# Seven block products in place of eight for x·w1, and sums that start from x in PSUM

## The chip, the cores and the metric

The kernel runs on one core of one Trainium2 chip. The metric is device microseconds of one execution; a single core runs it, so it is also the slowest core. Lower is better.

## The reference, cut to what matters

One transformer layer with two parallel branches on the same normalised input, all in fp32: S = 2048 tokens, D = 576, a hidden width F of 4608, 32 heads of 18.

```python
xn = layernorm(x)
q, k, v = split_heads(xn @ wqkv)                 # 576 -> 3 * 576
logits[s, w] = q[s] . k[s - 2 * w] * scale       # w = 0..7, masked where s - 2 * w < 0
A = (softmax(logits) @ v[s - 2 * w]) @ wo
B = relu(xn @ w1) @ w2                           # 576 -> 4608 -> 576
out = x + A + B
```

Nearly all of the multiplications are in `xn @ w1` (called h below), `relu(h) @ w2` (the second product), q/k/v and wo.

## The kernel before

**Precision.** Every fp32 operand of a matmul is split in two numbers of TensorE's format (fp32r): a high part, a copy that ScalarE makes, and a low part, the rest, subtracted by VectorE (helper `two`, L144). A product is then three products: high·high, high·low, low·high. D = 576 is four blocks of 128 rows and 64 rows left over. The left-over rows' high and low parts stand above one another in one block of 128, so that they take two matmuls where a full block takes three. The 14 pairs of blocks are the list `TERMS` (L326).

**Tokens.** They are dealt out in two phases (even and odd tokens), each of 8 tiles of 128, or 4 blocks of 256. A tile of x is loaded, normalised (`stats`, `norm`), turned on TensorE and split (`make_xt`, `transpose_split`); four tiles of the second phase are turned on VectorE and through DRAM instead (`norm_turned`, `xt_a`, `xt_f`, `xt_s`).

**The main loop** (L771) goes over `slots` (L540): phase, chunk of three F tiles (C = 3, 12 chunks), token block, F tile; 288 slots in all. In a slot:

- `h_mm` makes h for one F tile and one token block two slots ahead (LAG = 2): 14 matmuls of 128x128 by 256 tokens into a PSUM bank. `h_out` (L556) writes relu's high part by ScalarE (L563) and its low part by VectorE (L566) to SBUF.
- `o_mm` (L584) is the second product: for each of the two token tiles three products by two column halves (256 and 320 columns), so 12 matmuls, which accumulate over the three F tiles of a chunk in PSUM.
- After the third F tile `o_out` adds the PSUM sum to x in SBUF on VectorE (L620). After the last chunk the tile goes out.

All matmuls of the main loop are recorded at the helper `mm`, L113, and told apart by the tile that they write: `ph` is h, `po` the second product, `pm` q/k/v and wo (and a few others).

**Weights** are loaded on SP's queue to staging tiles and split ahead of use (`w1_task`, `w2_task`, `wq_tasks`, `wo_tasks`, `split_task`, `run_splits`; splits at L148 and L152); w1 and w2 are read from DRAM once per phase.

**Attention.** In four units of 8 heads per phase, `qkv_tile` runs 14 matmuls of 432 columns per token tile into `pm`, and ScalarE copies k, v and q out (L397 to L399). The first 7 places of k and v come from the neighbouring partition by DMA (the halo, L403). The rest of a unit is VectorE work in long instructions of 1152 columns (L428, L431, L458, L465), put in a queue `bg` and given out between other VectorE work by `run_bg` (L483), which compares two running sums of estimated PE and VectorE time. The result is turned on VectorE and through DRAM (`wo_a`, `wo_f`), split (`wo_s`), multiplied by wo (`wo_b`: 28 matmuls per token tile into `pm`) and added to x on VectorE (L529).

**Order of the work.** There is no scheduler at run time: each engine runs its instructions in program order and waits by semaphores. The program order is written out by hand for the head (L693 to L768) and follows from tables of slot numbers after that (`todo`, `todo_late`, `plan`). At the start h_terms runs the first products in pieces, as the parts of x and w1 become ready, and GpSimd makes some of the low parts (`by_pool`).

Of the kernel before, what the change touches and what calls it, by code (L numbers as in the profile page):

```python
# [17 lines left out]
P = 128  # L18
NPH = 2
NI = 8  # L20
NTB = 4
# [4 lines left out]
C = 3  # L26
LAG = 2
EPS = 1e-5

UNIT0, UNIT_STEP, WO_AT = 7, 26, 12  # L30

XT_STEPS = (
    (-6, 0, 1, 2, 4, 7),
    (-5, 1, 2, 3, 5, 8),
    (-3, 2, 3, 4, 6, 10),
    (3, 4, 5, 6, 8, 11),
)
WO_STEPS = (0, 1, 3, 4, 6, 7, 9, 10)
HEADW = (-9, -8, -7, -6, -5, -4)
FIRST = 4  # L40

HEAD = (
    (4, 0, 'stats', 6, False, True),
    (4, 1, 'norm', 6, True),
    (4, 1, 'stats', 7),
    (4, 1, 'norm', 7),
    (5, 1, 'xt', 6),
    (6, 0, 'xt', 7),
)
HALVED = 5  # L50
HALO = ((0, 112), (112, 127))
WARM = 24


@with_exitstack
def tile_body(ctx: ExitStack, tc: tile.TileContext, x, wqkv, wo, w1, w2, out):
# [5 lines left out]
    NF = F // P  # L62
    NCH = NF // C
    KT = 4
# [4 lines left out]
    SPC = NTB * C  # L69
    SPP = NCH * SPC  # L70
# [3 lines left out]
    consts = pool("consts", 1)  # L74
    xp = pool("xp", 11)
    xtp = pool("xtp", NTB)
    qop = pool("qop", 1)
    kp = pool("kp", 1)
    vp = pool("vp", 2)
    w1p = pool("w1p", C + 1)  # L80
    w2p = pool("w2p", C + 1)
    wqp = pool("wqp", 1)
    stp = pool("stp", 5)
    hp = pool("hp", LAG + 2)
# [3 lines left out]
    tmp = pool("tmp", 2)  # L88
    turned = pool("turned", 4, space=bass.MemoryType.DRAM)
    ps_o = pool("ps_o", 2, space=PSUM)  # L90
    ps_h = pool("ps_h", 2, space=PSUM)
    ps_m = pool("ps_m", 2, space=PSUM)

    f32 = lambda ap: ap.bitcast(F32)

    ident = consts.tile([P, P], F32, name="ident")
    make_identity(nc, ident)
    mhalf = consts.tile([P, 1], F32, name="mhalf")
    nc.gpsimd.memset(mhalf, -0.5)
    spare = consts.tile([P, 1], F32, name="spare")  # L100

    warm = ps_o.tile([P, 2, 512], F32, name="po")
    for _ in range(WARM):
        nc.tensor.transpose(warm[:, 0, 0:P], ident, ident)
# [3 lines left out]


    t = {"pe": 0.0, "dve": 0.0}  # L110

    def mm(o, l, r, start, stop, n):
        nc.tensor.matmul(o, l, r, start=start, stop=stop)  # L113
        t["pe"] += n / 2400.0 + 0.002

    def dve(n):
        t["dve"] += (n + 130) / 960.0


    tasks = deque()  # L120
    staged = deque()
    AHEAD = 3

    def split_task(step, load, split):
        tasks.append((step, load, split))

    def stage_more(ahead=AHEAD):
        while tasks and len(staged) < ahead:
            step, load, split = tasks.popleft()
            st = stp.tile([P, 640], F32, name="st")  # L130
            load(st)
            staged.append((step, split, st))

    def run_splits(n):
        nonlocal step_now
        while staged and staged[0][0] <= n:
            step_now, split, st = staged.popleft()
            split(st)
            stage_more()

    by_pool = set()
    step_now = None

    def two(hi, lo, src, n):  # L144
        if step_now == HEADW[0]:
            nc.vector.tensor_copy(hi, src)
        else:
            nc.scalar.activation(hi, src, AF.Copy)  # L148
        if step_now in by_pool:
            nc.gpsimd.tensor_tensor(lo, src, f32(hi), op=ALU.subtract)  # L150
        else:
            nc.vector.tensor_tensor(lo, src, f32(hi), op=ALU.subtract)  # L152
            dve(n)

    W1, W2, WQ, WO = {}, {}, {}, {}

    def w1_task(step, key, f):
        def load(st):
            c = slice(f * P, (f + 1) * P)
            nc.sync.dma_start(  # L160
                st[:, 0:512].rearrange("p (k c) -> p k c", k=KT),
                w1[0 : KT * P, c].rearrange("(k p) c -> p k c", p=P),
            )
            if key == (0, 0, 0):
                nc.scalar.dma_start(st[0:DR, 512:640], w1[KT * P : D, c])
                load_x(0, 1)
                nc.scalar.dma_start(st[DR:P, 512:640], w1[KT * P : D, c])
                return
            nc.sync.dma_start(st[0:DR, 512:640], w1[KT * P : D, c])
            nc.sync.dma_start(st[DR:P, 512:640], w1[KT * P : D, c])  # L170

        def split(st):
            w = w1p.tile([P, 2, 5 * P], F32R, name="w1t")
            two(w[:, 0, :], w[:, 1, :], st[:, :], 640)
            W1[key] = w

        split_task(step, load, split)

    def w2_task(step, key, f):
        def load(st):  # L180
            nc.sync.dma_start(st[:, 0:D], w2[f * P : (f + 1) * P, :])

        def split(st):
            w = w2p.tile([P, 2, D], F32R, name="w2t")
            two(w[:, 0, :], w[:, 1, :], st[:, 0:D], D)
            W2[key] = w

        split_task(step, load, split)

    def wq_tasks(steps, key, g):  # L190
        src = wqkv.rearrange("r (s c) -> r s c", s=3)

        def one(kt):
            def load(st):
                v = st[:, 0 : 3 * UD].rearrange("p (s c) -> p s c", s=3)
                c = slice(g * UD, (g + 1) * UD)
                if kt < KT:
                    nc.sync.dma_start(v, src[kt * P : (kt + 1) * P, :, c])
                else:
                    nc.sync.dma_start(v[0:DR], src[KT * P : D, :, c])  # L200
                    nc.sync.dma_start(v[DR:P], src[KT * P : D, :, c])

            def split(st):
                if kt == 0:
                    WQ[key] = wqp.tile([P, 10, 3 * UD], F32R, name="wq")
                w = WQ[key]
                two(w[:, kt, :], w[:, 5 + kt, :], st[:, 0 : 3 * UD], 3 * UD)

            return load, split

        for kt, step in enumerate(steps):
            split_task(step, *one(kt))

    def wo_tasks(steps, key):
        def one(kt):
            def load(st):
                if kt < KT:
                    nc.sync.dma_start(st[:, 0:D], wo[kt * P : (kt + 1) * P, :])
                else:
                    nc.sync.dma_start(st[0:DR, 0:D], wo[KT * P : D, :])  # L220
                    nc.sync.dma_start(st[DR:P, 0:D], wo[KT * P : D, :])

            def split(st):
                if kt == 0:
                    a = wqp.tile([P, 7, D], F32R, name="wq")
                    b = vp.tile([P, 3, D], F32R, name="v")
                    WO[key] = [a[:, k, :] for k in range(7)] + [b[:, k, :] for k in range(3)]
                w = WO[key]
                two(w[kt], w[5 + kt], st[:, 0:D], D)

            return load, split

        for kt, step in enumerate(steps):
            split_task(step, *one(kt))


    X, XT, XN, MR = {}, {}, {}, {}

    def load_x(ph, i):
        X[ph, i] = xp.tile([P, D], F32, name="x")  # L240
        if ph == i == 0:
            for c in slice(0, D2), slice(D2, D):
                nc.sync.dma_start(X[ph, i][:, c], x_v[ph, i][:, c])  # L243
            return
        (nc.scalar if (ph, i) == (0, 1) else nc.sync).dma_start(X[ph, i], x_v[ph, i])

    def stats(ph, i, parts=False, act=False):
        xt = X[ph, i]
        st = smp.tile([P, 2, 6], F32, name="bst")
        mv = smp.tile([P, 2], F32, name="mv", bufs=4)  # L250
        r = smp.tile([P, 1], F32, name="rstd", bufs=4)
        nm = smp.tile([P, 1], F32, name="nm", bufs=4) if act else mv[:, 0:1]
        MR[ph, i] = nm, r

        def sums():
            for h in range(2):
                nc.vector.bn_stats(st[:, h, :], xt[:, h * D2 : (h + 1) * D2])  # L257

        def rest():
            nc.vector.bn_aggr(mv, st)  # L260
            nc.vector.tensor_scalar(mv[:, 1:2], mv[:, 1:2], EPS, None, op0=ALU.add)
            if act:
                nc.gpsimd.tensor_scalar(nm, mv[:, 0:1], -1.0, None, op0=ALU.mult)
            nc.gpsimd.tensor_tensor(r, mv[:, 1:2], mhalf, op=ALU.pow)  # L264
            dve(700)

        if not parts:
            sums()
            rest()
        return sums, rest  # L270

    def norm(ph, i, act=False):
        nm, r = MR.pop((ph, i))
        xn = tmp.tile([P, 640], F32, name="xn", bufs=3)[:, 0:D]
        if act:
            nc.scalar.activation(xn, X[ph, i], AF.Identity, bias=nm)
            nc.scalar.activation(xn, xn, AF.Copy, scale=r)
        else:
# [4 lines left out]
    def transpose_split(src, hi, mix, lo, bank=None, parts=False):  # L283
# [28 lines left out]
        if not parts:  # L312
            for f in steps:
                f()
# [499 lines left out]
```

## Time and profile before

| | |
|---|---|
| Time, median of 3 runs | 1166.88 us (1165.29 to 1167.15) |
| Span of the profiled execution | 1163.8 us; no time of its own is listed, the median of the runs is 3.1 us more |
| Mean granted TensorE clock | 0.999 |
| Busy PE, VectorE (DVE), ScalarE (ACT), GpSimd (POOL) | 1155.9, 822.9, 308.1, 44.9 us |
| Bytes moved by DMA | 88.66 MB, mean 76 GB/s |

The span runs from the first to the last instruction of the profiled execution; what lies around it is in the time but not in the profile. PE stands for TensorE's matmuls and PEld for its weight loads, which overlap them. Several matmuls are in flight at once, so the mean length of one (277 ns for h) is longer than the distance from one to the next; paces are taken from runs of matmuls in the chain of work that ended last. A ScalarE or VectorE instruction overlaps the next one of its engine by about 0.1 us in the same way.

### The profile page before, as it was taken

The numbers are of one execution on the slowest core, as the hardware profiler recorded it, in microseconds if no ns is written. First come the engines' busy times: TensorE is split into PE (matmuls) and PEld (weight loads), VectorE is DVE, ScalarE is ACT, GpSimd is POOL, SyncE is SP. The second block draws the span as 40 slices with busy tenths as digits, with TensorE's granted clock in tenths as the row PEclk, the third lists the DMA queues.
The fourth block names the chain that finished last, engine by engine and source line by source line (L and its number), as shares of the span: only waits on it lengthen the run. The fifth ranks groups of instructions, "written<-read, shape, count | busy, mean of one in ns | idle before, by whom it ended". The sixth has DMA issues, their size and how long they took to land.

```text
span 1163.8 us, 21695 instructions
## 1 busy us (share of the span) xinstructions
PE 1155.9 (99%) x8916; PEld 1147.9 (99%) x8916; DVE 822.9 (71%) x1300; ACT 308.1 (26%) x747; POOL 44.9 (4%) x60
## 2 busy tenths in 40 slices
PE   8999999999999999999999999999999999999998
PEld 8999999999999999999999999999999999999998
DVE  7427885887687688876683288768858877887843
ACT  4422222131231212322433123222222312222210
POOL 2200100010000000000010001000100000000000
PEclk9999999999999999999999999999999999999999
DMA  6303221140321211365752113021312303113541
GB/s 184 98 23 85 65 55 53 40 112 1 94 76 34 82 32 52 96 151 116 175 170 66 46 53 94 22 77 36 92 34 62 110 1 101 44 32 97 123 100 63
DMA packets 149732, 88.66 MB, mean 76 GB/s; under 512 B 58512, under 2 KB 133264, under 8 KB 149632
## 3 DMA queue, kind: packets, MB, share of 16 engines
q1 hardware_dynamic: 146656, 78.54, 25.1%
q10 hardware_dynamic: 2976, 8.72, 2.6%
q8 instruction: 70, 1.15, 0.4%
q14 instruction: 30, 0.25, 0.1%
HBM read 67.90 MB, written 11.14 MB: 68 GB/s over the span
## 4 chain that ended last, share of the span: by engine, by line
PE 99%; issue 0%; DVE 0%; DMA 0%; POOL 0%; ACT 0%; SPq 0%; DVEq 0%; POOLq 0%
PE ph L113 39%; PE po L113 38%; PE pm L113 20%; PE pm L293 0%; DMA x<-in_x 0%; DVE x L626 0%; POOL rstd L264 0%; PE pm L294 0%; PE po L293 0%; ACT xT L298 0%; DVE xn L279 0%; DVE bst L257 0%; SPq L243 0%; DVEq L810 0%; PE ph L294 0%
## 5 line engine op out<-in xcount | busy, mean ns | idle before, releaser
L113 PE MATMUL ph<-xT,w1t 128*128 128x256 f32 x4018 | 505.0, 277 | 0.7 <-ACT xT L298 0.7
L113 PEld LDWEIGHTS ph<-xT,w1t 128*128 128x128 f32 x4018 | 486.8, 188 | 1.3 <-ACT xT L298 1.0
L113 PE MATMUL po<-w2t,hhi 128*128 128x256 f32 x2292 | 393.0, 293 | 0.0
L113 PEld LDWEIGHTS po<-w2t,hhi 128*128 128x128 f32 x2292 | 335.4, 188 | 1.1
L563 ACT ACTIVATE hhi<-ph 128x256 fp32r<-128x256 f32 x287 | 110.0, 384 | 582.2 <-PE ph L113 568.9
L113 PE MATMUL po<-w2t,hlo 128*128 128x256 f32 x1146 | 242.4, 292 | 0.0
L566 DVE SCALAR_TENSOR_TENSOR hlo<-ph,hhi 128x256 fp32r<-128x256 f32 x287 | 121.0, 422 | 164.5 <-ACT hhi L563 164.0
L113 PEld LDWEIGHTS po<-w2t,hlo 128*128 128x128 f32 x1146 | 188.9, 187 | 0.0
L620 DVE TENSOR_TENSOR x<-po,x 128x576 f32<-128x576 f32 x190 | 143.1, 757 | 60.1 <-PE po L113 57.2
L113 PE MATMUL pm<-wq,xT 128*128 128x432 f32 x896 | 185.5, 358 | 0.0
L113 PEld LDWEIGHTS pm<-wq,xT 128*128 128x128 f32 x896 | 163.8, 188 | 5.6
L428 DVE TENSOR_TENSOR pr<-qo,k 128x1152 f32<-128x1152 f32 x64 | 86.1, 1349 | 0.0
L431 DVE TENSOR_REDUCE lg<-pr 128x64 f32<-128x1152 f32 x64 | 85.1, 1343 | 0.0
L458 DVE TENSOR_TENSOR pr<-lg,v 128x1152 f32<-128x1152 f32 x64 | 84.7, 1350 | 0.0
L152 DVE TENSOR_TENSOR w2t<-st,w2t 128x576 fp32r<-128x576 f32 x72 | 55.8, 775 | 32.4 <-ACT w2t L148 32.3
L152 DVE TENSOR_TENSOR w1t<-st,w1t 128x640 fp32r<-128x640 f32 x70 | 58.9, 841 | 20.6 <-ACT w1t L148 20.5
L465 DVE TENSOR_TENSOR pr<-pr 128x288 f32<-128x288 f32 (+1 forms) x128 | 70.6, 601 | 0.0
L148 ACT ACTIVATE w2t<-st 128x576 fp32r<-128x576 f32 x72 | 49.3, 684 | 44.9 <-PE po L113 32.5
L397 ACT ACTIVATE k<-pm 128x144 f32<-128x144 f32 x64 | 18.7, 292 | 146.3 <-PE pm L113 146.3
L148 ACT ACTIVATE w1t<-st 128x640 fp32r<-128x640 f32 x71 | 52.1, 734 | 11.7 <-DMA k<-k 6.0
L434 POOL TENSOR_SCALAR_AFFINE_SELECT lg<-lg 1x512 f32<-1x512 f32 x8 | 9.9, 1234 | 809.6 <-DVE lg L431 809.6
L529 DVE TENSOR_TENSOR x<-pm,x 128x256 f32<-128x256 f32 (+1 forms) x32 | 13.1, 453 | 30.2 <-PE pm L113 30.2
(85 smaller groups left out, 470.0 us busy)
## 6 DMA issues: line engine op xcount, KB each, us to landing
st<-in_w SPq DMA_DIRECT2D x72, 288.0 KB, 3.1
st<-in_w SPq DMA_DIRECT2D x72, 256.0 KB, 3.2
st<-in_wqkv SPq DMA_DIRECT2D x32, 216.0 KB, 3.0
turned<-tr SPq DMA_DIRECT2D x64, 80.0 KB, 3.0
xn<-turned SPq DMA_DIRECT2D x16, 320.0 KB, 3.2
st<-in_w SPq DMA_DIRECT2D x142, 32.0 KB, 2.9
out<-x SPq DMA_DIRECT2D x15, 288.0 KB, 2.1
x<-in_x SPq DMA_DIRECT2D x14, 288.0 KB, 4.3
```

The lines of the kernel that those rows point to most:

```text
L113: nc.tensor.matmul(o, l, r, start=start, stop=stop)
L148: nc.scalar.activation(hi, src, AF.Copy)
L152: nc.vector.tensor_tensor(lo, src, f32(hi), op=ALU.subtract)
L397: nc.scalar.activation(k[:, W - 1 + i, :], pq[:, 1, :], AF.Copy)
L428: nc.vector.tensor_tensor(pr[i], q, window(k, i), op=ALU.mult)
L431: nc.vector.tensor_reduce(lg[:, i], pr.pop(i).rearrange(heads, d=Dh), axis=AX.X, op=ALU.add)
L458: nc.vector.tensor_tensor(pr[i].rearrange(heads, d=Dh), e, window(v, i).rearrange(heads, d=Dh), op=ALU.mult)
L465: nc.vector.tensor_tensor(o, z[:, 0:n], z[:, n : 2 * n], op=ALU.add)
L529: nc.vector.tensor_tensor(acc, po[h], acc, op=ALU.add)
L563: nc.scalar.activation(hi, pt, AF.Relu)
L566: nc.vector.scalar_tensor_tensor(lo, pt, 0.0, f32(hi), op0=ALU.max, op1=ALU.subtract)
L620: nc.vector.tensor_tensor(acc, whole, acc, op=ALU.add)
```

## The change

The work per phase is now 18 pairs of F tiles by two halves of the tokens (`G`: 72 groups in all). A group is 256 F columns by 512 tokens.

**h.** For a group, w1's 512 full rows are two halves of 256, and its 256 columns two F tiles; x's tokens are two blocks of 256. That is a product of 2x2 blocks. In all but the first four groups it is made by a Strassen (Winograd) scheme: seven products of sums of blocks, P1 to P7, instead of eight. The sums of w1's blocks (T1 to T4) are made for each pair by VectorE, the sums of x's blocks (S1 to S4) once for each phase and half. Partial results go on from product to product: P5 and P3 add up in bank bk3; P1, P6, P7 and P4 in bank bk2, which ScalarE copies to bank bkA after P1, where P2 adds to it, and to SBUF (SN2) after P6. P7's and P3's results are added to SBUF copies by VectorE. The 64 left-over rows are multiplied in the plain way, 2 matmuls for each of the four outputs, on top of P5, P2, P3 and P4. The first four groups (`classic`) are as before, 14 matmuls for each F tile and token block.

**Second product and wo.** For each token tile the sum over a pair's two F tiles (and, in four pairs of each phase, over a unit's part of wo) starts from x, which ScalarE has copied to PSUM, and ScalarE copies it back to SBUF after it. VectorE's adds of L620 and L529 go. wo's share of a unit is added when the unit is done (`WOP`), with the 16 left-over rows of each unit gathered and added with the last.

**Weights.** w1, w2, wqkv and wo are first copied within DRAM on GpSimd's queue, per pair or unit, and loaded from the copies. A pair's w1 blocks and sums take one of two SBUF buffers; in the pairs of `QP` the other one holds the q/k/v weights, and the next pair's w1 blocks are loaded and split after the last q/k/v matmul (`set_make` with `fine`).

**x of the second phase** is loaded to the attention's scratch tiles, normalised and turned on TensorE in groups 34 and 35, and split and summed in groups 35 and 36.

**Order.** A planner (`Order`) runs while the program is built: it keeps an estimated clock for each engine, and gives out ScalarE's and VectorE's instructions in the order in which they can start by these estimates, earliest due first. Attention instructions wait in a queue of their own and are placed on VectorE where they end at most 0.6 us after the start of the next known instruction. Each PE step forces what it needs.

The core of the diff:

```diff
+    def pick(self, eng):
...
+        if eng == DVE and self.back:
+            op = self.back[0]
+            r = self.ready(op)
+            if r is not None:
+                s = max(now, r)
+                if soon is None or s + op.dur <= soon[1] + self.SLACK:
+                    return op, s
+        return soon
...
+    def s_forms(h, slack):
...
+        a1 = dve(lambda: sub(z[S1], z[S3], z[S1], ALU.add), 512, [*RAW[h, 1], *XOK[h, 1]], slack)
+        a3 = dve(lambda: sub(z[S3], z[S2], z[S3]), 512, [a1, *raw, *XOK[h, 0]], slack + 0.6)
+        a2 = dve(lambda: sub(z[S2], z[S1], z[S2]), 512, [a3], slack + 1.2)
+        a4 = dve(lambda: sub(z[S4], z[S4], z[S2]), 512, [a2], slack + 1.8)
...
+    def terms(bank, ws, xs, start):
+        o = bank[:, 0:TBN]
+        for j, (wp, xp_) in enumerate(((0, 0), (0, 1), (1, 0))):
+            for k in range(len(ws[0])):
+                mm(o, ws[wp][k], xs[xp_][k], start and j == k == 0, False)
+
+    def rest(bank, m, f, xr):
+        w = wset(m)
+        for e in range(2):
+            mm(bank[:, 0:TBN], w[:, e, RR, f], xr, False, e == 1)
...
+    def pstep(g, name):
...
+        if name == "P5":
+            def f():
+                terms(bk3, slot(m, T1), sform(h, S1), True)
+                rest(bk3, m, 1, XR[h][:, 1])
+
+            t = pe(f, T8, [*ok[T1], *ok[RR], *XOK[h, "s"], *XOK[h, 1], *BANK["bk3"]])
+            BANK["bk3"] = [act(lambda: copy(SN5, b3), TBN, [t, *SNF[5]], 3)]
+        elif name == "P1":
+            t = pe(lambda: terms(bk2, slot(m, B11), aform(h, 0, 0), True), T6, [*ok[B11], *XOK[h, 0], *BANK["bk2"]])
+            BANK["bk2"] = [act(lambda: copy(bA, b2), TBN, [t, *BANK["bkA"]], 0.4)]
...
+        elif name == "P4":
+            def f():
+                terms(bk2, slot(m, T4), aform(h, 1, 1), False)
+                rest(bk2, m, 0, XR[h][:, 1])
+
+            t = pe(f, T8, [*ok[T4], *BANK["bk2"]])
+            BANK["bk2"] = h_parts((g, 1, 0), b2, [t], 0.2)
...
+    def o_step(g, j, idx, k):
...
+        t = pe(f_, 0.26 * len(prods), [*ok, *POF[k]])
...
+        if seeded(g, j):
+            e = act(lambda: copy(X[i], whole(k)), D, [t], 0.5 + 0.3 * k)
...
+        if after[0] < NG:
+            i2 = 4 * G[after[0]][2] + 2 * after[1] + k
+            POF[k] = [act(lambda: copy(whole(k), X[i2]), D, [e, XLAST[i2]], 1.2 + k * (1.2 if j else 0.4))]
...
+    steps = ("P5", 0), ("P1", 0), ("P6", 0), ("P2", None), ("P7", 1), ("P3", 1), ("P4", None)
+    for g in range(2, NG + 1):
...
+        cnt = {"P5": l0 // 3, "P1": l0 - l0 // 3 - l0 // 4, "P6": l0 // 4, "P7": l1 // 2, "P3": l1 - l1 // 2}
+        for name, q in steps:
+            pstep(g, name)
+            tick(name)
+            if q is not None:
+                o(q, cnt[name])
```

`l0` and `l1` are the steps of the second product (and wo) of the group before, for its first and second token block; a step is six matmuls for one token tile and F tile. In a group without wo both are 4.

More of the change, by code (lines that the diff above doesn't have):

```diff
@@ L20 @@
 NI = 8
-NTB = 4
 TBN = 256
@@ L127, in stage_more @@
[L127 to L153, printed above, removed]
@@ L179, in w2_task @@
[L179 to L212, printed above, removed]
@@ L237, in tile_body, with copy @@
[L237 to L253, printed above, removed]
+    def copy(o, i, func=AF.Copy):
+        nc.scalar.activation(o, i, func)
@@ L405, in tile_body @@
-    bg = deque()
-    ready = set()
+            hi, lo = H[key]
+            nc.vector.scalar_tensor_tensor(lo, src, 0.0, f32(hi), op0=ALU.max, op1=ALU.subtract)
+        a = act(high, TBN, after, slack)
+        b = dve(low, TBN, [a], slack + 0.45)
+        HOK[key] = [a, b]
+        return [a, b]
+    def terms(bank, ws, xs, start):
[3 more added lines that the diff above has]
+                mm(o, ws[wp][k], xs[xp_][k], start and j == k == 0, False)
```

1368 lines of the change are left out of this document (862 added, 506 removed).

## The prediction

> **What bounds the kernel now.** First the page's head, busy shares, slices and chain.
>
> ```profile
> span 1163.8 us, 21695 instructions
> PE 1155.9 (99%) x8916; PEld 1147.9 (99%) x8916; DVE 822.9 (71%) x1300; ACT 308.1 (26%) x747; POOL 44.9 (4%) x60
> ...
> PE   8999999999999999999999999999999999999998
> ...
> PEclk9999999999999999999999999999999999999999
> ...
> PE 99%; issue 0%; DVE 0%; DMA 0%; POOL 0%; ACT 0%; SPq 0%; DVEq 0%; POOLq 0%
> ```
>
> TensorE (PE) is busy at full granted clock, and the chain that ended last is PE alone. A busy PE may still be a slow PE, so second the busy time by stretch, at both edges and one inside (columns: stretch, length, PE, PEld, DVE, ACT, POOL, clock, DMA share, GB/s):
>
> ```profile
> 0.00:16.00 16.00, 11.82 (x82) 10.85 (x82) 9.59 (x25) 8.04 (x15) 5.72 (x13) 1.00 0.84 247
> 16.00:100.00 84.00, 84.00 (x622) 82.96 (x621) 38.51 (x77) 25.46 (x70) 10.77 (x13) 1.00 0.25 71
> ...
> 1150.00:1163.80 13.80, 10.11 (x82) 9.91 (x80) 3.91 (x8) 0.77 (x2) 0.00 (x0) 0.94 0.24 87
> ```
>
> From 16 us on PE has no gap; all idle time is 4.2 us at the head and 3.7 at the tail. So a removed matmul is worth its pace (start to start), and any new gap is paid in full. Third, the paces, from the chain in order of time (start, length, what):
>
> ```profile
> 405.62 1.59 PE ph L113 x14
> 407.21 1.56 PE po L113 x12
> ...
> 41.62 2.73 PE pm L113 x14
> ...
> 508.21 3.65 PE pm L113 x28
> ```
>
> An h matmul (256 columns) takes 1.59/14 = 0.1136 us, one of the second product 1.56/12 = 0.130, one of q/k/v 2.73/14 = 0.195, one of wo 3.65/28 = 0.130. As a check, the code's counts: 4032 × 0.1136 + 3456 × 0.130 + 896 × 0.195 + 448 × 0.130 = 1140 us, with 60 transposes and the warm-up the PE row.
>
> **The change, part by part.** *h on PE.* Before, two F tiles by two token blocks cost 4 × 14 = 56 matmuls. Now such a group takes seven products of 3 × 2 = 6 matmuls, and the 64 left-over rows 2 for each of 4 outputs: 42 + 8 = 50. Of 2 × 18 × 2 = 72 groups four stay plain (28 matmuls per F pair and block twice, 56). So 68 × 6 = 408 matmuls go: 408 × 0.1136 = **-46.3 us**. The second product keeps 72 × 48 = 3456 matmuls, wo 448, q/k/v 896. All 16 x tiles are now turned on PE, where 12 were: 20 more transposes.
>
> ```profile
> 15.46 0.60 PE L293 MATMUL pm<-ident,xn 128*128 128x128 f32 x4
> ...
> 15.89 0.27 PE L294 MATMUL ph<-ident,xn 128*64 128x128 f32 x1
> ```
>
> Four start within 15.89 - 15.46 = 0.43, so 20 × 0.11 = **+2.2 us**. PE's own work falls by 44.1: with all else as it was, the span is 1119.7.
>
> *What moves to ScalarE and VectorE.* Rows of their costs (busy and mean ns), then, from the order of time, a release chain and back-to-back starts:
>
> ```profile
> L563 ACT ACTIVATE hhi<-ph 128x256 fp32r<-128x256 f32 x287 | 110.0, 384 | 582.2 <-PE ph L113 568.9
> ...
> L566 DVE SCALAR_TENSOR_TENSOR hlo<-ph,hhi 128x256 fp32r<-128x256 f32 x287 | 121.0, 422 | 164.5 <-ACT hhi L563 164.0
> L620 DVE TENSOR_TENSOR x<-po,x 128x576 f32<-128x576 f32 x190 | 143.1, 757 | 60.1 <-PE po L113 57.2
> ...
> L428 DVE TENSOR_TENSOR pr<-qo,k 128x1152 f32<-128x1152 f32 x64 | 86.1, 1349 | 0.0
> ...
> L148 ACT ACTIVATE w2t<-st 128x576 fp32r<-128x576 f32 x72 | 49.3, 684 | 44.9 <-PE po L113 32.5
> ...
> L529 DVE TENSOR_TENSOR x<-pm,x 128x256 f32<-128x256 f32 (+1 forms) x32 | 13.1, 453 | 30.2 <-PE pm L113 30.2
> ```
> ```profile
> 98.36 0.38 ACT L563 ACTIVATE hhi<-ph 128x256 fp32r<-128x256 f32 x1 [2.77 <-PE ph L113]
> 98.65 0.73 ACT L148 ACTIVATE w1t<-st 128x640 fp32r<-128x640 f32 x1
> ...
> 104.95 0.68 ACT L148 ACTIVATE w2t<-st 128x576 fp32r<-128x576 f32 x1
> 105.53 0.73 ACT L148 ACTIVATE w1t<-st 128x640 fp32r<-128x640 f32 x1
> ```
> ```profile
> 405.46 1.76 PE L113 MATMUL ph<-xT,w1t 128*128 128x256 f32 x14
> ...
> 407.05 0.68 PE L113 MATMUL po<-w2t,hhi 128*128 128x256 f32 x4
> 407.25 0.38 ACT L563 ACTIVATE hhi<-ph 128x256 fp32r<-128x256 f32 x1 [0.91 <-PE ph L113]
> ...
> 407.67 0.42 DVE L566 SCALAR_TENSOR_TENSOR hlo<-ph,hhi 128x256 fp32r<-128x256 f32 x1 [0.53 <-ACT hhi L563]
> ```
>
> The 190 VectorE adds of L620 go, and wo's 32 with them (-143 and -13 us, none on the path). In their place, two token tiles at a time, ScalarE copies the PSUM sum to SBUF and then writes the next tile's x into PSUM: 72 × 8 less 4 = 572 copies of 576 columns at 0.68 = 389 us of ScalarE. The scheme adds three ScalarE copies of 256 (68 × 3 × 0.38 = 78) and two VectorE adds (136 × 0.42 = 57) per group; the weight sums four VectorE subtractions per pair (136 × 0.42 = 57), and the weight splits grow from 1280 to 2048 columns per pair (about +35 each). With some 20 for sums of x, ScalarE goes from 308 to about 830 us of 1130, VectorE from 823 to about 840. Both stay under PE, so they cost only where PE must wait for one.
>
> *Steady group.* PE runs P5, o, P1, o, o, P6, o, P2, P7, o, o, P3, o, o, P4, where o is six matmuls (0.78), P1, P6, P7 take 0.68, the others, with 8 matmuls, 0.91: 11.9 us. After PE's slot ScalarE starts 0.20 later (407.25 - 407.05), VectorE 0.04 after ScalarE's end, and ScalarE takes its next instruction 0.29 after a 256 copy, 0.58 after a 576 one. The waits that PE gets, each against the work between:
> - P6 needs P1's copy out of the same bank: 0.20 + 0.38 + 0.05 = 0.63, cover two o = 1.56.
> - P7 needs P6's copy: 0.63, cover o + P2 = 1.69.
> - P1 of the next group needs P4's high part (ScalarE) and then low part (VectorE): 0.20 + 0.38 + 0.04 + 0.42 + 0.05 = 1.09, cover P5 + o = 1.69: slack 0.60, the smallest.
> - An o of the next token pair needs copy and x in PSUM: 0.20 + 0.58 + 0.68 + 0.05 = 1.51, cover P6 + o + P2 + P7 = 3.05 inside a group and o + P4 + P5 = 2.60 across the edge. Both token tiles plus P4's high part queue there: 4 × 0.58 + 0.29 = 2.6 within the 4.06 until the second tile is due.
> - P3's add frees its bank in 0.67 against two o and P4 = 2.47.
>
> Hence a steady group has no stall by itself. But a 1.35 us attention instruction that VectorE has just begun adds up to 1.27 (its pace) to the smallest slack, so up to 0.67 per group. Attention has 192 such instructions, 250 us or 22% of the time; over half of the hits outlast the slack, by 0.33 on average: 0.22 × 0.53 × 0.33 × 68 = 2.6 us. With collisions of weight splits on ScalarE I take **+4.5** (0 to 15).
>
> ScalarE writing into PSUM has no row. I take 0.68 from the nearest, the 576 copy within SBUF; below it stands 0.38, the 256 copy (the count of columns excludes less), above it twice 0.68, priced as a rival.
>
> *Weights.* Each pair's set is loaded, summed and split one pair ahead, except after the 7 pairs whose buffer holds q/k/v weights. There six loads wait on SP for the last q/k/v matmul, with the k and v halo copies behind them. PE has P6, P2, P7, P3, P4 and five o, 8.0 us, before P5 needs the first sum.
>
> ```profile
> st<-in_w SPq DMA_DIRECT2D x72, 256.0 KB, 3.2
> ...
> x<-in_x SPq DMA_DIRECT2D x14, 288.0 KB, 4.3
> ```
>
> Issue 0.5, landing 3.2, subtraction 0.42, high 0.38, low 0.42 make 5.0; the left-over rows follow 1 us later. Cover 2 us: no cost; without it 3 us each. Copies in DRAM (POOL's queue) have no row; they start two groups, 24 us, ahead of use, against 2 to 5 us for landings here. I take 0.
>
> *Head.* The first h product ran in pieces as x and weights became ready; it now waits for both x tiles and the split weights whole.
>
> ```profile
> 10.29 3.73 PE ph L113 x28
> ```
>
> VectorE must first do two tiles' statistics and one normalisation, four low parts of x and five of weights that POOL helped with before: 2 to 3 us later than 10.29. After that VectorE needs some 2.9 us per x tile and PE has 3.2 to 6 us of work between. **+3** (0 to 7).
>
> *Change of phase.* x of the second half is split and summed while group 35 runs, and P5 of groups 36 and 37 waits for the last form. That is 8 us of VectorE for each (two splits of 1024 and one of 512 columns for x, four sums of 512, two splits of 1024 for the sums), beside 5 for the next x tiles and 4.5 of usual work, in 14.6 us of PE: 3 late at 36, 1 at 37: **+4** (0 to 8). *Tail*: the last copy takes 576 columns at once: +0.3.
>
> **Sum.** 1163.8 - 46.3 + 2.2 + 4.5 + 3 + 4 + 0.3 = 1131.5 of span. No separate time is shown for the profiled execution; the median of the runs shown, 1166.88, is 3.1 above the span. So **1134.6 us**.
>
> **Rivals.**
> - *Slower: VectorE in front of P4's low part.* If nearly every group catches a long attention instruction there, 0.67 × 68 = 46 us come back: 1134.6 - 4.5 + 46 = 1176. For it: 2.8 such instructions per group, and the low part becomes known to the planner only once its high part is placed. Against: long groups (q/k/v, wo) have more cover, and the planner lets a background instruction run over a known one by 0.6 at most. It decides from (44.1 - 7.3)/68 = 0.54 us per group.
> - *ScalarE's PSUM writes cost double.* Then the second tile's x lands 0.2 to 0.3 late per group: about 18 us, 1148. For it: no row. Against: reading PSUM is not dear (256 in 0.38). The Trainium skill, ScalarE: Activation LUTs, Step-by-step: what each stage is for, goes further against it: ScalarE's writes reach PSUM sooner than SBUF. No row here shows such a write, so the case keeps a chance.
> - *Sets late after q/k/v.* 7 × 3 = 21 us: 1155. For it: x loads took 4.3 in the busy head. Against: DMA share 0.25.
> - *PE's granted clock drops.* If one group in ten ran its h matmuls at half rate, 7 × 5.7 = 40 us: 1174, slower. Against it: the clock row reads 9 throughout, across the 4.2 us without work at the head too. The Trainium skill, TensorE: Matmul & The Clock Gate, A second HAM failure mode: psum-queue depth-cycling, tells of a kernel cycling through PSUM banks whose small pauses made the clock fall and rise again; no row here shows it.
> - *Nothing stalls.* Head, phase change and groups as before: 1119.7 + 3.1 = 1123.
>
> **How the numbers follow.** Forecast 0.68; nothing stalls 0.10; dear PSUM writes 0.07; late sets 0.05; VectorE in front 0.08; clock 0.02. From 1122 to 1153 lie the first three, 0.85: the low end is 1123 less 1 for reading errors, the high end 1122.8 + 15 + 7 + 8. Faster by over 0.2% (what a measurement of this kernel can tell from no change): 0.68 + 0.10 + 0.07 + 0.05 = 0.90; slower 0.08 + 0.02 = 0.10. One hundredth of each goes to mixtures of stalls that land near zero: 0.89, 0.02 and 0.09.
>
> **What would show it.** The page after should count 8916 - 408 + 20 = 8528 PE instructions. PE's idle time, by stretch, should be 4 + 3 us at the head, about 4 near the change of phase and a few us spread over the rest. The 576 copies into PSUM should read near 0.68, ScalarE busy near 830, VectorE near 840. Wrong would be: many PE waits on a low part or on x in PSUM (over 0.2 us per group), gaps of 3 us seven times, a lower clock, or another pace than 0.1136.

## The result, and the profile after

| | before | after |
|---|---|---|
| Time, median of 4 runs each | 1167.02 us | 1201.03 us (1199.90 to 1201.66) |
| Span of the profiled execution | 1163.8 us | 1199.9 us (its own time 1201.66) |
| Ratio | | 1.0293, 95% interval 1.0279 to 1.0308 |

The changed kernel is 34 us slower where 32 us less was forecast, and its time lies above the range as well (1122 to 1153). In every execution that lists both, the time is 1.7 to 1.9 us more than the span. So the profiled execution of before took about 1165.6 us, and the two spans are 36 us apart. The executions of before differ by up to 4 us, with the granted clock: those at 0.999 and above took 1165.0 to 1165.9 us, those at 0.998 and below 1166.5 to 1169.0.

The profile after begins with these lines: busy us, share of the span, count of instructions; then the granted clock by fortieths of the span.

```profile
PE 1162.5 (97%) x8528; PEld 1140.0 (95%) x8528; DVE 826.4 (69%) x1533; ACT 743.0 (62%) x1658; POOL 64.2 (5%) x97
...
PEclk8999999999999999899999999999999999999999
```

The count is the one forecast, 8528. So PE has 388 instructions fewer and is busy 6.6 us longer. Its busy share of 97% hides how, because a PE whose matmuls follow one another more slowly is still busy. Two things have to be read apart: the distance from one matmul's start to the next (the pace), and the gaps, where that distance is over 60 ns longer than its usual value. The gaps hold the waits, and also the matmuls that run while the granted clock is low.

**Gaps.** Here are the windows of both kernels. Columns: the stretch in us, its length, busy us (count) of PE, PEld, DVE, ACT and POOL, granted clock, DMA share, GB/s. First before:

```profile
0.00:60.00 60.00, 55.82 (x413) 54.30 (x414) 35.93 (x83) 25.83 (x59) 16.49 (x26) 1.00 0.47 137
...
340.00:400.00 60.00, 60.00 (x428) 59.17 (x427) 45.08 (x71) 14.48 (x44) 2.86 (x3) 1.00 0.20 58
```

And after:

```profile
0.00:60.00 60.00, 48.91 (x293) 45.22 (x293) 41.30 (x93) 32.92 (x80) 15.17 (x30) 0.91 0.65 208
...
340.00:400.00 60.00, 53.52 (x380) 52.16 (x379) 41.67 (x82) 32.99 (x70) 5.86 (x10) 0.94 0.49 143
...
450.00:500.00 50.00, 46.47 (x341) 45.62 (x340) 43.53 (x65) 28.88 (x62) 3.82 (x6) 0.93 0.37 115
...
560.00:660.00 100.00, 95.77 (x728) 93.66 (x727) 64.14 (x137) 71.51 (x150) 11.74 (x18) 1.00 0.38 121
660.00:1160.00 500.00, 496.15 (x3680) 488.76 (x3679) 356.82 (x647) 315.99 (x714) 9.80 (x10) 1.00 0.25 68
```

Before, PE idled at the head only. After, it idles at the head, in two stretches (at 350 to 390 and at 490 us), near the change of phase, and a little everywhere; at the head and in the two stretches the clock falls too. Added up from the starts of all matmuls in the trace, the gaps are 6.6 us before and 60.4 after, by stretch: head (0 to 60) 17.7 against 6.2; 340 to 400 and 450 to 500 together 18.3 against 0; 560 to 660 7.2 against 0.3; all the rest 17.2 against 0.1. About 8 us of the 60.4 are matmuls at a granted clock of 0.50: 3 in the head and 5 in the two stretches.

**Pace.** In the prediction's rows of before, 14 h matmuls run from 405.46 to 407.05 (1.59 us) and an o, six matmuls of the second product, in 0.78. The same in the timeline of after (start, us, engine, line, operation, count):

```profile
77.21 1.58 PE L276 MATMUL bk<-xa,wset 128*128 128x256 f32 x12
...
78.86 1.57 PE L276 MATMUL bk<-xa,wset 128*128 128x256 f32 x12
...
82.16 0.72 PE L276 MATMUL po<-w2t,hhi 128*128 128x256 f32 x4
...
82.98 0.69 PE L276 MATMUL po<-w2t,hhi 128*128 128x256 f32 x4
...
83.78 1.57 PE L276 MATMUL bk<-xa,wset 128*128 128x256 f32 x12
```

14 h matmuls take 78.86 - 77.21 = 1.65, an o 0.82 and 0.80: nothing waits here, and the matmuls are 3 to 5% slower. Over the whole trace h went from 113.9 to 118.0 ns and a second-product pair (a matmul of 256 columns and one of 320) from 119.8 + 141.0 to 118.1 + 148.6. The sum over all matmuls is 26.3 us.

**The account of the span:** 1163.8 - 46.3 (matmuls left out) + 2.2 (transposes) + 26.3 (pace) + 53.8 (gaps) = 1199.8, against 1199.9 measured. The experiments are about the last two terms; the paces and gaps that they give are counted from all matmul starts of each trace in the same way.

### The profile page after: what moved, and what is told of

Its sections match the earlier page's. It is cut to its first block, busy times and chain, and to the rows that moved or that the text cites. A ratio compares the mean times of both kernels' runs of the same rounds, so it can differ in the third digit from the quotient of the medians.

```text
span 1199.9 us, 21930 instructions
## 1 busy us (share of the span) xinstructions
PE 1162.5 (97%) x8528; PEld 1140.0 (95%) x8528; DVE 826.4 (69%) x1533; ACT 743.0 (62%) x1658; POOL 64.2 (5%) x97
## 4 chain that ended last, share of the span: by engine, by line
PE 73%; DVE 12%; ACT 8%; issue 3%; DMA 3%; POOL 0%; SPq 0%; ACTq 0%; DVEq 0%; POOLq 0%
PE po L276 32%; PE bk L276 21%; PE pm L276 14%; PE bkA L276 5%; DVE wset L273 3%; ACT po L270 2%; ACT x L270 2%; DVE ts L273 2%; DMA olo<-turned 1%; DVE hlo L554 1%; ACT wset L270 1%; DVE sn L273 1%; ACT hhi L270 1%; DVE pr L870 1%; DVE pr L840 1%
## 5 line engine op out<-in xcount | busy, mean ns | idle before, releaser
L276 PE MATMUL po<-w2t,hhi 128*128 128x256 f32 (+1 forms) x2304 | 407.1, 299 | 6.1 <-ACT po L270 5.9
L276 PE MATMUL po<-w2t,hlo 128*128 128x256 f32 (+1 forms) x1152 | 248.1, 297 | 0.0
L276 PE MATMUL bk<-xs,wset 128*128 128x256 f32 x1632 | 238.2, 282 | 7.0 <-DVE sn L273 7.0
L270 ACT ACTIVATE x<-po 128x576 f32<-128x576 f32 x286 | 182.2, 644 | 100.3 <-PE po L276 97.6
L276 PEld LDWEIGHTS bk<-xs,wset 128*128 128x128 f32 x1632 | 217.7, 189 | 8.1 <-DVE sn L273 7.8
L270 ACT ACTIVATE po<-x 128x576 f32<-128x576 f32 x286 | 187.0, 654 | 2.9
L276 PE MATMUL pm<-wset,xa 128*128 128x432 f32 x768 | 172.9, 360 | 2.6 <-ACT wset L270 1.5
L276 PEld LDWEIGHTS pm<-wset,xa 128*128 128x128 f32 x768 | 140.2, 188 | 9.9 <-ACT qo L270 2.3
L276 PE MATMUL bk<-xa,wset 128*128 128x256 f32 x924 | 138.7, 288 | 7.5 <-DVE hlo L554 4.8
L276 PEld LDWEIGHTS bk<-xa,wset 128*128 128x128 f32 x924 | 125.8, 193 | 13.2 <-DVE hlo L554 10.1
L273 DVE TENSOR_TENSOR wset<-wset 128x512 fp32r<-128x512 f32 (+2 forms) x120 | 70.8, 599 | 11.9 <-ACT wset L270 11.5
```

Source lines behind the costliest of these rows:

```text
L270: nc.scalar.activation(o, i, func)
L273: nc.vector.tensor_tensor(o, a, b, op=op)
L276: nc.tensor.matmul(o, l, r, start=start, stop=stop, skip_group_check=True)
```

## The experiments

The first question was the pace. Theory A: the change moved buffers, and the pace hangs on where operands lie in SBUF. Theory B: busier ScalarE, VectorE and DMA slow TensorE's reads. For the two long stretches, theory C: the DRAM copies on GpSimd's queue come in bursts.

**e1_map** measures the matmuls alone, with both operands at every multiple of 64 bytes within 512, and nothing else running.

```diff
+ for m in M: for w in WT: kind_h(m, w, b)   # 24 matmuls of 256 columns
+ for w in WT: for m in M: kind_o(m, w, b)   # 12 of 256 and 12 of 320, alternating
```

> This kernel computes nothing of the layer: it only runs blocks of 24 matmuls with no other engine at work, in the two shapes of h (256 columns, four blocks in turn) and of the second product (256 and 320 columns). Eight moving and eight stationary tiles start at all multiples of 64 bytes within 512. Theory A (the pace of a matmul depends on where its operands lie in SBUF): h at 0.113 to 0.114 where moving and stationary lie as before the change (448 and 256 within 512), 0.117 to 0.119 where they lie as after (moving 192, stationary 0 to 192); a pair of the second product at 0.260 where the moving operand lies at 0 or 256, at 0.266 elsewhere. Theory B (the slower pace comes from what the other engines do at the same time, ScalarE's writes to PSUM above all): one pace everywhere, 0.114 and 0.260.

Its timeline, blocks of 24 matmuls, three of h and then five of the second product. The left name is the moving operand: ma lies at 128 (mod 512), mb at 192, mc at 256, md at 320, me at 384. The right one is the stationary: wa at 128, wc at 256, we at 384, wf at 448, wg at 0.

```profile
29.39 3.05 PE L86 MATMUL pox<-ma,we 128*128 128x256 f32 x24
32.28 2.89 PE L86 MATMUL poy<-ma,wf 128*128 128x256 f32 x24
35.01 3.00 PE L86 MATMUL pox<-ma,wg 128*128 128x256 f32 x24
...
199.50 3.36 PE L94 MATMUL pox<-ma,wa 128*128 128x256 f32 x24
202.71 3.28 PE L94 MATMUL poy<-mb,wa 128*128 128x256 f32 x24
205.82 3.28 PE L94 MATMUL pox<-mc,wa 128*128 128x256 f32 x24
208.94 3.33 PE L94 MATMUL poy<-md,wa 128*128 128x256 f32 x24
212.11 3.36 PE L94 MATMUL pox<-me,wa 128*128 128x256 f32 x24
...
249.92 3.36 PE L94 MATMUL pox<-ma,wc 128*128 128x256 f32 x24
253.12 3.33 PE L94 MATMUL poy<-mb,wc 128*128 128x256 f32 x24
```

A pair takes (202.71 - 199.50)/12 = 267 ns where the two operands lie at the same place modulo 256 bytes (wa, stationary, less ma, moving), 259 and 260 at a distance of 192 and 128, 264 at 64. The distance is not all: of the 32 blocks at 128 or 192, 26 took 260, two 264 and four 267, as ma with wc does here ((253.12 - 249.92)/12, at a distance of 128). h takes 2.89/24 = 120 ns at distance 0 and 2.73/24 = 114 at 64, but at ten of fifteen places of that distance it took 118, as it did at 128 and 192. All the paces of both kernels are here with no other engine at work, so theory B isn't needed. By the addresses that the two programs give their buffers, the second product's operands were 128 apart in before and 0 in after. The Trainium skill, TensorE: Matmul & The Clock Gate, section Step-by-step: what each phase is for, says that the two operands come through two independent read ports of SBUF, so that loading one doesn't take bandwidth from the other. The bandwidth may not be shared, but the pace isn't independent: these rows differ in nothing but the two addresses.

**e2_before_shift** moves all buffers of before by 128 bytes.

```diff
+    consts.tile([P, 32], F32, name="pad")
```

> The kernel before, with one unused tile of 128 bytes behind the identity, so that nearly all operands lie 128 bytes further on: moving operands of the second product at 128 and 384 within 512 instead of 256 and 0, x at 64 instead of 448, w1 at 384 instead of 256. No instruction changes. Theory A: the pace of after, 1952 pairs by 6 ns and 4032 matmuls by 3 to 5 ns, 12 + 12 to 20 us longer: 1191 to 1199. Theory B: 1167, unchanged.

Measured: 1165.34 us, ratio 0.9992 (0.9983 to 1.0002), the paces as they were. So A, as it was put, missed: the places all moved, the distances and the paces didn't. The map doesn't foretell h here: it has 118 ns for h at these places (md with we), and the run kept 113.9.

**e6_before_rel** changes the distance of the second product's operands in before from 128 to 0. That of most of wo's matmuls goes with it; h's and nearly all of q/k/v's stay.

```diff
     w2p = ...
+    pool("gap", 1).tile([P, 32], F32, name="gap")
     hp = pool("hp", LAG + 2)
```

> The kernel before with 128 unused bytes between w2's tiles and the tiles of h's parts, so that the distance of the two operands of the second product becomes 0 within 256 bytes instead of 128, as it is after the change; h's operands stay as they were. Theory A2: 1728 pairs by 6.6 ns, 11 us longer: 1177 to 1180. Theory B: 1167.

Measured: 1196.86 us, ratio 1.0254 (1.0240 to 1.0268). 128 unused bytes cost 30 us. Its timeline:

```profile
1177.23 0.70 PE L114 MATMUL po<-w2t,hhi 128*128 128x256 f32 x4
...
1178.84 1.81 PE L114 MATMUL ph<-xT,w1t 128*128 128x256 f32 x14
1180.49 0.70 PE L114 MATMUL po<-w2t,hhi 128*128 128x256 f32 x4
```

Two o take 1.61 in place of 1.56, as the map says. But 14 h matmuls take 1.65 in place of 1.59 (117.8 ns over the whole run), and h's own operands weren't moved apart. That is why it cost nearly three times the 11 us expected: a matmul's pace hangs on the other matmuls of the stream too. These are also the two paces of after (the sum is 29 us here, 26.3 there). The other engines do here what they do in before, so B falls, and layout alone is enough for the pace term, without the scheme.

**e3_after_sp** takes the DRAM copies off GpSimd's queue.

```diff
-  nc.gpsimd.dma_start(W1C[n], ...)      # and W2C, WQC, WOC
+  nc.sync.dma_start(W1C[n], ...)
```

> The changed kernel with the copies of w1, w2, wqkv and wo within DRAM issued on SP's queue instead of GpSimd's; all else is in the same order. Theory C (copies queue up behind GpSimd's instructions that wait for VectorE and ScalarE, then go out in bursts that delay the small loads to 7 or 8 us): the three pauses of 2 to 3 us near 351, 386 and 490 us go, and the slow clock behind them; 14 to 18 us less than the changed kernel, near 1184. Rival (the loads are late because of the traffic as such, or SP's own waits hold the copies up as much): 1195 or more.

First what it undoes, in after: GpSimd's timeline.

```profile
337.52 1.10 POOL L846 TENSOR_SCALAR_AFFINE_SELECT lg<-lg 1x512 f32<-1x512 f32 x1 [85.40 <-DVE lg L843]
338.58 0.51 POOL L401 DMA_DIRECT2D w2c<-in_w  x1
...
340.66 0.50 POOL L401 DMA_DIRECT2D w2c<-in_w  x1
```

Four copies that are due one by one (two of them in the lines left out) stand behind an attention instruction for which GpSimd waits 85 us, and then go out together. ScalarE's and PE's timelines of after, and its windows there:

```profile
351.17 0.42 ACT L270 ACTIVATE ohi<-olo 128x256 fp32r<-128x256 f32 x1 [5.48 <-DMA olo<-turned]
```
```profile
354.04 0.97 PE L276 MATMUL bk<-xs,wset 128*128 128x256 f32 x6 [2.73 <-DVE sn L273]
```
```profile
346.00:350.00 4.00, 4.00 (x33) 4.00 (x32) 1.51 (x4) 0.00 (x0) 0.00 (x0) 1.00 0.97 347
...
352.00:354.00 2.00, 0.00 (x0) 0.00 (x0) 2.00 (x5) 0.00 (x0) 0.00 (x0) 1.00 0.32 93
354.00:356.00 2.00, 1.49 (x10) 1.28 (x11) 2.00 (x5) 1.95 (x4) 0.00 (x0) 0.99 0.59 173
356.00:358.00 2.00, 2.00 (x10) 1.88 (x10) 2.00 (x6) 1.35 (x4) 0.00 (x0) 0.50 0.00 0
358.00:360.00 2.00, 2.00 (x12) 2.00 (x12) 2.00 (x3) 0.07 (x1) 0.00 (x0) 0.65 0.00 0
```

The burst fills the DMA engines (0.97). A load of 128 KB that usually lands in 2.7 us takes 8.2. ScalarE stands before its use for 5.48 us, with everything behind it; PE then idles for 2.7 us. It starts again at 354.04 at the full clock, and from 356 on the granted clock is 0.50 and 0.65. The Trainium skill, TensorE: Matmul & The Clock Gate, section What's actually happening, has the clock halve after an idle window of about 3.4 us. The trace agrees in kind, with a pause shorter than that, 2.7 us.

Measured in e3_after_sp: 1184.45 us, ratio 1.0144 (1.0127 to 1.0161); C holds, for 16.6 us. Its windows:

```profile
0.00:60.00 60.00, 50.61 (x299) 46.77 (x300) 41.02 (x93) 32.93 (x80) 7.69 (x18) 0.94 0.32 99
340.00:400.00 60.00, 59.85 (x443) 59.12 (x442) 42.65 (x85) 35.88 (x82) 0.93 (x1) 1.00 0.39 101
```

PE is whole again at 340 to 400; with 450 to 500 the gaps are 1.5 us where they were 18.3. The head's gaps hardly change (16.2 us, 17.7 in after) although its DMA share fell from 0.65 to 0.32: the copies aren't what holds the head.

**e4_after_align** and **e5_align_sp** give the changed kernel distances as the map wants them, the second also with e3's edit.

```diff
+    pool("gap", 1).tile([P, 32], F32, name="gap")          # behind w2p
+    keep.tile([P, 16], F32, name="pad")                    # ahead of BUF
-    BUF = [keep.tile([P, 10 * 3 * UD], ...
+    BUF = [keep.tile([P, 2 * 2176], ...                    # q/k/v parts as a list of slices
```

> The changed kernel with three pads in SBUF, no instruction changed: the stationary operands of the second product now lie 128 bytes (within 256) behind the moving ones instead of 0, and all of w1's 64 behind x's instead of 0, 64, 128 and 192. Theory A2 (the distance of the two operands within 256 bytes sets the pace, as in the map: 0 costs 267 ns a pair, 128 costs 260; h 113.3 at x 192 and w1 0 or 256): 1952 pairs by 6.6 ns and some 3500 h matmuls by 4.5 ns, 28 us less than the changed kernel: 1170 to 1178. Theory B (other engines slow the matmuls): 1201.

> The pads of e4 and the copies on SP's queue of e3 together. If the two causes are independent, 1184.5 - 28 = 1156 to 1158, faster than the kernel before; if taking PE's slack away by a faster pace turns into waits for ScalarE and VectorE, 1165 or more.

Measured: 1189.89 us (ratio 1.0194, 1.0177 to 1.0212) and 1171.60 us (1.0044, 1.0032 to 1.0057). h goes to 114.9, the pair to 262.3 ns; the pace term falls from 26.3 to 6.9 us over before, so in the changed kernel too most of it was layout. But e4 got 11 of its 28 us and missed its range, and e5 falls under the second case, 1165 or more: the gaps rise, from 60.4 to 67.2 and from 43.4 to 50.5, most of it outside the head and the two stretches. So 7 of 19 us come back as waits: faster matmuls run up against ScalarE and VectorE.

**e7_slack0** is e5 with the planner's allowance for a background instruction that runs over a known one taken away (0.6 to 0).

> As e5, but the planner places an attention instruction on VectorE only where it ends before the next known instruction can start, not up to 0.6 us after it. Theory D (the waits of PE for a low part, 10 us in e3, come from attention instructions that VectorE has just begun): 4 to 8 us less than e5. Rival (the low part is not yet known to the planner when the attention instruction is placed, so the limit does not act on it): within 2 us of e5.

Measured: 1170.08 us, ratio 1.0026 (1.0016 to 1.0037), 1.5 us less, as the rival says. The allowance hardly matters.

**e8a_distance** and **e8b_order** start from e7. The first puts 192 bytes between the second product's operands instead of 128, the second changes the order of the products as well.

```diff
-    steps = ("P5", 0), ("P1", 0), ("P6", 0), ("P2", None), ("P7", 1), ("P3", 1), ("P4", None)
+    steps = ("P1", 0), ("P5", 0), ("P6", 0), ("P2", None), ("P7", 1), ("P4", 1), ("P3", None)
```

> The changed kernel with its buffers moved as in e5_align_sp, the copies issued by SyncE, the planner's slack at 0, and the gap behind the second weights' pool now 192 bytes in place of 128, which makes the distance of the second product's two operands 192 in place of 128 (mod 256). Theory of the distance: the pair of second-product matmuls goes from 261.6 ns to 259.4-260 ns, so some 1,600 pairs give 2 to 4 us: 1166-1168 us. Rival (distance no longer decides once it is not 0, or what matmuls save comes back as waits for P4's low part and for seeds): within 1.5 us of the 1170.1 us of the kernel with 128.

> As e8a_distance, and the order of the block products is P1, P5, P6, P2, P7, P4, P3 in place of P5, P1, P6, P2, P7, P3, P4, so that VectorE has the matmuls of P4 and P3 between the last add of P7 and the operand of the next pair's first product, and P4's low part is no longer made right behind P7's sums. Theory that the remaining waits are waits for VectorE's chain in front of P4: TensorE's waits for P4's low part (8.4 us in 17 waits) fall below 3 us, and the run takes 4 to 8 us less than e8a_distance, about 1158-1163 us, below the kernel before. Rival: the chain's work per pair is unchanged, so the waits appear in front of the next operand or of a seed: within 2 us of e8a_distance.

Measured: 1172.57 us (ratio 1.0049, 1.0037 to 1.0062) and 1189.15 us (1.0190, 1.0175 to 1.0204). Both lie above both of their cases. In e8a h rose from 114.8 to 116.3 ns with its own operands where they were, and the pair rose from 262 to 263: a map of uniform blocks doesn't foretell a stream in which two kinds of matmuls alternate. In e8b the waits for a low part are gone, but others grew. The rows are waits of PE's weight loads (PEld), which run ahead of the matmuls, so PE itself loses less: in e7, 4.3 us in 13 times for the low part. First e7 (e8a is like it: 8.7 us in 18 and 7.9 in 17), then e8b (us in total, times, longest):

```profile
PEld bk L279 <- DVE hlo L557: 8.4, 17, 1.1
PEld po L279 <- ACT po L273: 8.1, 16, 0.9
```
```profile
PEld po L279 <- ACT po L273: 18.4, 32, 1.3
...
PEld bk L279 <- ACT sn L273: 5.6, 4, 1.5
PEld bk L279 <- DVE sn L276: 4.7, 4, 3.1
```

The waits moved to the x in PSUM, to the copies of a bank and to the adds.

**e9_all_four** adds 64 bytes to e7 so that all four operands stand as in before, modulo 256.

```diff
+    pool("gap0", 1).tile([P, 16], F32, name="gap0")
     w2p = pool("w2p", 4)
```

> The kernel of e7_slack0 with 64 unused bytes ahead of the second weights' pool, so that all four operands of the matmuls (x sums, first weights, second weights, h) stand at the places modulo 256 bytes that they have in the kernel before: 192, 0, 0 and 128. Theory that the pace is set by the places of all four against each other (the two of h, the two of the second product, and the one pair against the other): the matmuls take the paces of the kernel before, 260.5 ns a pair in place of 261.4 and 113.9 ns for h in place of 114.7; by some 1,700 pairs and 3,400 of h that is 4 us less, 1166 us, level with the kernel before. Rival (the distance within each pair of operands is all that counts, and it is unchanged here; or the new form of the kernel has a pace of its own): 1170 us, paces as in e7_slack0.

Measured: 1171.93 us, ratio 1.0048 (1.0034 to 1.0062), no gain. Its timeline shows two paces, in two places:

```profile
676.16 0.68 PE L280 MATMUL po<-w2t,hhi 128*128 128x256 f32 x4
...
676.94 0.68 PE L280 MATMUL po<-w2t,hhi 128*128 128x256 f32 x4
...
677.72 0.85 PE L280 MATMUL bk<-xa,wset 128*128 128x256 f32 x6
...
844.93 0.69 PE L280 MATMUL po<-w2t,hhi 128*128 128x256 f32 x4
...
845.72 0.70 PE L280 MATMUL po<-w2t,hhi 128*128 128x256 f32 x4
...
846.52 1.74 PE L280 MATMUL pm<-wset,xa 128*128 128x432 f32 x8
```

The stream of matmuls has two rhythms. At 676 us an o takes 0.78, matmul by matmul 120 and 140 ns, which is before's pace to the nanosecond, and h runs at 113 and 114. At 844 us the same matmuls at the same addresses take 0.79 and 0.80, with 117 and 147 to 153, and h 117 to 119. A rhythm lasts up to tens of us. In three stretches of the longer one (724 to 760, 842 to 888, 979 to 1015) wo's or q/k/v's matmuls lie between, in two of the shorter (660 to 677, 778 to 789) none; that these bring the longer rhythm on was not tried. Of the 320-column matmuls 13% are over 143 ns in before, all in after, nearly all in e6, 60% in e7, 44% in e9. So the theory of the four places gives the shorter rhythm right, but not how often the stream keeps it. What sets the rhythm stays open, and with it the last 6 to 9 us of the pace term.

**e10_halved** is e7 with VectorE's long attention instructions cut in two.

```diff
-  nc.vector.tensor_tensor(pr[i], q, window(k, i), op=ALU.mult)
+  nc.vector.tensor_tensor(pr[i][:, HALF[z]], q, window(k, i)[:, HALF[z]], op=ALU.mult)
```

> The kernel of e7_slack0 with the 192 attention instructions of 1152 columns on VectorE (the products with k, their sums, the products with v) each made as two of 576, the same work in 384 pieces of 0.75 us in place of 192 of 1.35 us. Theory (the prediction's: a long attention instruction that VectorE has just begun holds up P4's low part): TensorE's waits for a low part, 8.4 us in 17 waits, fall below 3 us, and with the seeds behind them the run gets 4 to 7 us shorter, 1163-1166 us, a little under the kernel before. Rival (the low part is late because ScalarE's high part is, or because VectorE has too much to do as a whole; the split adds about 5 us to VectorE's work): the waits stay within 2 us and the time within 1.5 us of 1170.

The mechanism that it tests, in after: VectorE's, ScalarE's and PE's timelines.

```profile
930.31 1.35 DVE L840 TENSOR_TENSOR pr<-qo,kk 128x1152 f32<-128x1152 f32 x1
931.58 0.42 DVE L554 SCALAR_TENSOR_TENSOR hlo<-bk,hhi 128x256 fp32r<-128x256 f32 x1
```
```profile
930.52 0.38 ACT L270 ACTIVATE hhi<-bk 128x256 fp32r<-128x256 f32 x1
```
```profile
932.05 0.50 PE L276 MATMUL bk<-xa,wset 128*128 128x256 f32 x2 [0.28 <-DVE hlo L554]
```

The high part is there at 930.90, VectorE is in an attention instruction until 931.6, and PE gets the low part 0.28 late. Measured with the halves: 1167.99 us, ratio 1.0012 (1.0003 to 1.0021). The waits of e10:

```profile
PEld po L279 <- ACT po L273: 15.7, 24, 1.1
PEld bk L279 <- DVE hlo L557: 4.8, 8, 1.3
```

Low-part waits fell from 17 to 8, which the rival excludes, but to 4.8 us and not below 3; the waits for x in PSUM doubled, which neither case has. So 2 us remain of 4 to 7. This is the best version that was run, and it is within 0.2% of before: 1163.8 - 46.3 + 2.2 + 5.7 (pace) + 40.6 (gaps) = 1166.0, the span measured.

## Why the prediction was wrong

The forecast span was 1131.5, the measured one 1199.9. The 68.4 us between them are 26.3 of pace, 18.3 of the two stretches behind the DRAM copies, and 12.6, 8.5 and 2.9 by which the steady groups, the head and the change of phase exceeded their terms.

- **Counts and sizes held.** 8528 PE instructions, so -46.3 and +2.2 stand. The 3.1 from span to time should have been about 1.8, which is what the executions with both figures show. The write of x into PSUM took 0.654 where 0.68 was taken, the copy out 0.644; VectorE was 826 busy against 840, ScalarE 743 against 830. The rivals of dear PSUM writes and of late sets are out. These are the groups of after (busy, mean ns; idle before):

```profile
L270 ACT ACTIVATE x<-po 128x576 f32<-128x576 f32 x286 | 182.2, 644 | 100.3 <-PE po L276 97.6
...
L270 ACT ACTIVATE po<-x 128x576 f32<-128x576 f32 x286 | 187.0, 654 | 2.9
```

- **The step that failed first: "PE's pace carries over", +26.3 us.** The sum priced each matmul left at before's 0.1136 and 0.130, though the change lays out every large buffer anew. "Another pace than 0.1136" was named among the signs of an error and had no price and no chance. Shown: in e6 the whole term appears in before through 128 unused bytes, and in e4 other addresses take 19 of the 26 us away from the changed kernel.
- **The DRAM copies, taken at 0, cost 17.** The cover (two groups ahead) was counted from the place in the program. The queue that they were moved to was not read: GpSimd's instructions ahead of them wait up to 85 us. Shown: e3.
- **Steady groups: +4.5 forecast (0 to 15), 17.1 measured.** The mechanism was right in kind: about 8 of the 17 us are gaps in front of a low part, and halving the attention instructions (e10) halves those waits. But 5 more are in front of x in PSUM, which the slacks, worked out one at a time on an undisturbed ScalarE, had put at nothing; and a wait hands itself on. e8b takes the low-part waits away, e10 halves them, and both get them back as waits for x in PSUM.
- **Head +3, measured 11.5; change of phase +4, measured 6.9.** Both in kind as foreseen, the head outside its range. Neither the copies (e3) nor the paces (e5) move the head by more than 2 us. The first h product starts at 12.15, 1.9 us later than before's 10.29, where 2 to 3 were forecast. About 3 us of the head's gaps are matmuls at half the clock (the next point); the rest is mostly waits of 1 to 3 us each (x's first forms and left-over rows, normalised x, weights), and which of them is the dear one was not tried.
- **The clock.** The rival of a lower clock asked for many small pauses. What came were a few long ones, at the copies' bursts and in the head. The prediction took it from before's head that 4.2 us without work don't lower the clock; in after's head, with pauses of 2.1 and 2.0 us, it fell:

```profile
0.00:16.00 16.00, 10.46 (x50) 9.44 (x51) 7.87 (x22) 7.59 (x18) 3.42 (x12) 0.74 0.92 301
```

  The clock was 0.50 from 7.8 to 18.1 us there. With the copies on SyncE's queue the slow stretches at 350 to 390 and 490 are gone and the mean clock is 0.997, but the head's remain. They are not the new scheme's alone: e6, whose instructions are before's, had 0.50 from 9.6 to 16.4. In all, half clock costs the changed kernel some 8 us.
- **The sign.** The mechanism of the slower rival (VectorE in front of P4's low part) was there at about a quarter of its price. What made the kernel slower was in no rival: 26.3 of pace and 17 of copies. Without the copies and with most of the pace term gone (e5, e7, e10) the change saves 46 us of matmuls and pays about as much in waits and what is left of the pace term (40.6 and 5.7 in e10). Whether a planner that also knew when x must be in PSUM could win some of it back stays open.

## What to carry to other kernels

When a change moves buffers, a matmul pace taken from the old layout is not a constant: compare the operands' distances modulo 256 bytes, avoid 0, and leave room for 3 to 4% in the range all the same, because the map's distances foretold neither h in e2 nor e8a. A transfer moved to another engine's queue goes out when the instruction ahead of it there is done, so read what that engine waits for. A slack of 0.6 us against instructions of 1.35 us isn't cover, and taking one such wait away passes it to the next link.

## What the runs showed of the hardware that was not expected

- With nothing else running, a pair of fp32r matmuls (256 and 320 columns) takes 259 to 267 ns, and one of 256 columns 114 to 120, by where the moving and the stationary operand lie in SBUF (e1). At distance 0 modulo 256 bytes a pair always took 266 to 267; at 128 or 192 it took 260 in 26 of 32 blocks.
- The pace of one kind of matmul depends on the other kind in the stream: h went from 113.9 to 117.8 ns when h's own operands stayed in place and the second product's were moved (e6). One stream at the same addresses has a shorter and a longer rhythm, each of which lasts up to tens of us (e9).
- Some pauses of TensorE of 2 to 3 us were followed by a granted clock of 0.50 for 3.4 us or more, which began within 2 us of the pause's end (after: pause 351.3 to 354.0, clock 0.50 from 356.0; e10: pause 24.9 to 27.1, clock 0.50 from 27.7). Others weren't: one of 2.2 us in after (27.1 to 29.4) and one of 1.8 in before (7.1 to 8.9).
